# Tile 3's first layer begun on six ranked heads, paired up blocks for single tiles, and a new emission order

## The chip, the cores and the metric

One NeuronCore of a Trainium2 chip runs the whole program. The metric is the device time of one execution in microseconds (us), the median of several runs. Engines: TensorE (PE; its weight loads stand as PEld), VectorE (DVE), ScalarE (ACT), GpSimd (POOL) and SyncE (SP), which here only issues DMAs.

## What is computed

A top-32 attention over 8 heads, followed by two dense layers of width 2048 with a softplus between the first pair of matrices and a leaky ReLU between the second. All in float32; the weights arrive as float64 bit patterns that the kernel turns into float32 itself.

```python
scores = scale * np.matmul(q, k.transpose(0, 1, 3, 2))          # B,H,S,D = 2,8,576,64
kth = np.partition(scores, -32, axis=-1)[..., -32:-31]
scores = np.where(scores >= kth, scores, -1e9)
attn = np.exp(scores - scores.max(-1, keepdims=True))
x = np.matmul(attn / (attn.sum(-1, keepdims=True) + 1e-9), v)    # to 1152 x 512
h = x @ w_in;  x = (np.maximum(h, 0) + np.log1p(np.exp(-np.abs(h)))) @ w_out      # 512 -> 2048 -> 512
h = x @ w_in2; out = (np.maximum(h, 0) + alpha * np.minimum(h, 0)) @ w_out2
```

## The kernel before

The 1152 rows of tokens are 9 tiles of 128. `CHUNKS` groups them as [3], [4], [5], [6, 7, 8], [0, 1, 2]; below these are chunks 0 to 4. Chunks 0 to 2 run the first layer one tile at a time and the second layer together (`TOGETHER`); in these stages (`NATIVE`) the matrix products run in plain float32, which the trace shows as two matmuls per product. Chunks 3 and 4 split each float32 into a high and a low part and run three matmuls per product (`three`).

Per row (a tile and one head): `scores` makes the products on PE and copies them out on ACT. `topk` ranks on DVE: four MAX8 (L480) and three MATCH_REPLACE8 (L483) of 576 columns find the 32nd largest; then ACT or DVE makes the mask (L508 to L511), POOL subtracts it (L514), ACT takes the exponential (L516). `flip` transposes on PE, `values` multiplies by v on PE. When a tile's eighth head is through, `finish` takes the reciprocal of the sums on DVE, spreads it over the columns (POOL L606, PE L604, ACT L609) and one DVE product (L612) writes the tile's features `x` (called "x of tile t" below). Only then can the tile's first layer start.

`Layer.up(j)` makes block j (of 16) of the first matrix on PE from the four 128-row parts of x (L652 where float32), then three ACT instructions (L663 to L665: abs, exp, ln) and one DVE instruction (L666) make the softplus `g`; `Layer.down(j)` accumulates g times the second matrix on PE (L698, 512 columns). `convert` turns one unit of weights (two blocks, 1 MB of float64) into float32: two loads by SP, two DVE instructions (L351, L354), two of ACT (L357), four of POOL (L360), and a store for later reuse. The raw data lie in a ring of `RAWB` buffers, so a load waits until the unit `RAWB` before it has passed POOL.

All of this is first collected as 3208 numbered operations (`plan`), and then emitted in the order of the hand-written table `ORDER`; each engine, and SP's DMA queue, works in that order. An entry `fN` of the table emits N filler products of the identity with itself (L785, two matmuls each, 128 columns) on PE, whose result nobody reads. The 242 fillers all stand ahead of the first `up` block. A letter b behind an entry picks the operation's second engine (DVE for POOL, or DVE for ACT).

Of the kernel before, what the change touches and what calls it, by code (L numbers as in the profile page):

```python
# [8 lines left out]
F32 = mybir.dt.float32  # L9
# [9 lines left out]
P = 128  # L19
# [28 lines left out]
RAWB = 2  # L48
RING = 15
NATIVE = {(0, 1), (0, 2), (1, 2), (0, 0)}  # L50
HOLD = {(0, 1): 2, (0, 2): 4}

# [99 lines left out]
4 2 3 5 12 364 363 386 387 240 f11 6 19 96 7 8 56 f3 9 195 95 11 10 156 40 77 f4 13 26 41 117 14 0 42 27 15 f3  # L152
16 28 18 43 17 365 79 366 80 29 367 44 370 30 368 388 369 31 45 371 403 f31 20 32 372 21 63 22 404 f3 23 33
373 64 25 389 24 34 f4 57 46 393 65 35 47 36 390 66 394 81 48 391 67 395 59 58 82 37 392 423 f19 60 68 49 1
422 38 61 83 396 62 50 39 258 69 51 119 70 120 f9 52 54 103 71 405 53 72 105 55 104 f8 78 406 73 84 410 106 74
85 411 407 107 412 f8 75 424 440 76 408 86 425 409 87 121 429 88 142 439 413 122 426 89 108 430 143 123 90 427
109 431 f27 91 124 93 428 92 459 110 94 432 f4 97 125 111 458 118 441 99 112 98 144 100 126 113 135 145 101
127 442 114 146 128 446 158 129 f11 115 147 159 443 447 160 448 148 102 130 444 181 476 116 149 445 f14 131
182 161 133 150 475 460 449 132 151 162 134 f8 136 461 152 157 163 462 203 465 183 463 164 464 137 204 184 138
466 494 153 f10 139 477 467 174 185 141 140 478 468 f4 154 495 165 479 186 155 226 480 166 205 481 227 187 482  # L160
167 511 206 168 188 483 169 207 484 189 242 f26 170 172 485 228 171 190 512 173 208 243 f4 175 191 229 196 177
197 496 192 198 497 176 199 f2 178 209 498 230 219 501 499 210 231 500 179 180 244 502 f11 193 211 530 200 513
503 194 265 201 514 212 266 504 531 245 515 232 213 518 202 516 246 f18 380 517 214 381 233 519 374 547 382
# [136 lines left out]
def topk_attention_moe_kernel(ctx: ExitStack, tc: tile.TileContext, q, k, v, w1, w2, w3, w4, alpha, out):  # L300
# [185 lines left out]
    def topk(i):  # L486
        ci, ti, t, h = rows[i]
        if h == 0:
            tiles[t]["sum"] = buf("sum", 2, [P, H], F32, f"sum{t}")
# [348 lines left out]
```

## Time and profile before

| | us |
|---|---|
| median of 3 runs (lowest, highest) | 666.4 (665.17, 666.89) |
| the profiled execution | 665.31 |
| its span, first to last instruction | 663.5 |
| PE busy / DVE busy / ACT busy / POOL busy | 646.6 / 543.2 / 496.7 / 376.0 |

The span is 1.8 us shorter than the execution's own time. A PE shown as busy may still be waiting between two matmuls, since ends of matmuls are modelled; where this matters, starts are compared with starts.

### The profile page before, as it was taken

To read this page: it belongs to the slowest core of one execution; us is meant where nothing else is said; L and a number is where in the kernel's file an instruction comes from. 1 tells how busy PE (TensorE), PEld (TensorE's weight loads), DVE (VectorE), ACT (ScalarE), POOL (GpSimd) and SP (SyncE) were. 2 spreads that over 40 slices of the span, in tenths; PEclk is the share of its full clock that TensorE was granted. 3 is DMA by queue.
4 is the path that set the end of the run, shared out by engine and by line. 5 is a ranking of instruction groups with operands and counts; after the bars stand their busy time and mean duration, and the time that the engine had idled before them with its cause. 6 is when DMAs were issued, how large, how long until landed. Compare 5 with 4: busy or idle time off the path is not lost.

```text
span 663.5 us, 12370 instructions
## 1 busy us (share of the span) xinstructions
PE 646.6 (97%) x4340; PEld 501.7 (76%) x4340; DVE 543.2 (82%) x1046; ACT 496.7 (75%) x1118; POOL 376.0 (57%) x402
## 2 busy tenths in 40 slices
PE   9999998999999899999999999999999999999997
PEld 7899865667667554555567878878988999999886
DVE  4999999999999999999998889999744654664632
ACT  4778799898799978888788889888554667763532
POOL 1567766651343667887675769887643443652520
PEclk9999999899999999999999999999999999999999
DMA  8776787740044378857615322221233434432401
GB/s 294 251 213 214 227 252 256 254 144 1 1 130 142 112 221 271 283 184 230 211 64 156 100 89 85 83 69 61 95 126 128 147 124 128 157 130 96 159 1 47
DMA packets 30014, 98.46 MB, mean 148 GB/s; under 512 B 3456, under 2 KB 3968, under 8 KB 29952
## 3 DMA queue, kind: packets, MB, share of 16 engines
q1 hardware_dynamic: 29952, 97.67, 45.1%
q8 instruction: 34, 0.56, 0.3%
q14 instruction: 28, 0.23, 0.1%
HBM read 78.52 MB, written 19.14 MB: 147 GB/s over the span
## 4 chain that ended last, share of the span: by engine, by line
PE 74%; DVE 7%; issue 5%; ACT 5%; POOL 5%; DMA 3%; SPq 0%; POOLq 0%; DVEq 0%
PE pa L698 8%; PE ph L624 7%; PE pa L624 7%; PE ph L625 7%; PE ph L626 7%; PE pa L625 7%; PE pa L626 7%; PE scrap L785 7%; PE ph L652 6%; PE pss L471 5%; PE pp L529 3%; POOL cx L360 3%; DMA cr<-in_w_dram 3%; DVE r L483 2%; DVE m L480 2%
## 5 line engine op out<-in xcount | busy, mean ns | idle before, releaser
L370 POOL TENSOR_TENSOR w<-w,wh 128x512 fp32r<-128x512 f32 x82 | 126.7, 1555 | 101.4 <-ACT wh L393 93.7
L514 POOL TENSOR_TENSOR e<-s,e 128x288 f32<-128x288 f32 x144 | 120.0, 854 | 62.6 <-ACT e L509 57.4
L480 DVE MAX8 m<-r 128x8 f32<-128x576 f32 x216 | 155.4, 745 | 0.1
L360 POOL TENSOR_TENSOR cx<-cx,cr 128x256 int32<-128x256 int32 x128 | 93.6, 756 | 68.3 <-ACT cr L357 66.7
L483 DVE MATCH_REPLACE8 r<-m,r 128x576 f32<-128x576 f32 x144 | 106.1, 740 | 0.0
L698 PE MATMUL pa<-cx,g 128*128 128x512 f32 x188 | 94.5, 613 | 3.0 <-DVE g L666 2.6
L357 ACT ACTIVATE cr<-cr 128x512 int16<-128x512 uint32 x64 | 82.6, 1378 | 7.8 <-DVE cr L354 7.6
L393 ACT CAST wh<-w 128x1024 fp32r<-128x1024 f32 x64 | 66.8, 1045 | 6.4 <-PE pa L624 2.0
L476 ACT COPY s<-pss 128x288 f32<-128x288 f32 x144 | 53.3, 407 | 20.3 <-PE pss L471 19.7
L785 PE MATMUL scrap<-ident 128*128 128x128 f32 x484 | 60.9, 283 | 1.4 <-POOL ident masks.py:199 1.4
L785 PEld LDWEIGHTS scrap<-ident 128*128 128x128 f32 x484 | 57.4, 196 | 6.3 <-issue 4.9
L480 DVE MAX8 m<-s 128x8 f32<-128x576 f32 x72 | 52.6, 747 | 11.3 <-ACT s L476 11.3
L516 ACT ACTIVATE e<-e,nb 128x576 f32<-128x576 f32 x72 | 55.7, 774 | 5.6 <-POOL e L514 5.4
L624 PE MATMUL pa<-w,gh 128*128 128x512 f32 x144 | 59.0, 409 | 0.0
L371 DVE TENSOR_TENSOR w<-w,wh 128x512 fp32r<-128x512 f32 x46 | 37.2, 811 | 25.7 <-ACT wh L393 24.2
L625 PE MATMUL pa<-wh,gl 128*128 128x512 f32 x144 | 56.8, 395 | 0.0
L626 PE MATMUL pa<-wh,gh 128*128 128x512 f32 x144 | 56.8, 395 | 0.0
L471 PE MATMUL pss<-ks,q 64*64 64x288 f32 x576 | 53.3, 428 | 2.5 <-ACT pt L532 2.4
L672 DVE SCALAR_TENSOR_TENSOR g<-g,rest,ph 128x384 f32<-128x384 f32 x48 | 29.1, 607 | 31.6 <-ACT g L670 31.5
L670 ACT ACTIVATE g<-ph 128x384 f32<-128x384 f32 x48 | 23.3, 487 | 42.3 <-PE ph L626 37.7
L371 DVE TENSOR_TENSOR gl<-g,gh 128x384 fp32r<-128x384 f32 x41 | 42.2, 1028 | 15.1 <-ACT gh L679 14.9
L652 PEld LDWEIGHTS ph<-xh,cx 128*128 128x128 f32 x336 | 42.5, 193 | 15.1 <-issue 9.2
(130 smaller groups left out, 1459.5 us busy)
## 6 DMA issues: line engine op xcount, KB each, us to landing
w<-ws SPq DMA_DIRECT2D x67, 512.0 KB, 3.3
cr<-in_w_dram SPq DMA_DIRECT2D x64, 512.0 KB, 5.4
ws<-cx SPq DMA_DIRECT2D x32, 512.0 KB, 6.5
v<-in_v_dram SPq DMA_DIRECT2D x12, 320.0 KB, 6.9
ks<-in_k_dram SPq DMA_DIRECT2D x11, 288.0 KB, 5.7
out_dram<-o SPq DMA_DIRECT2D x9, 256.0 KB, 2.1
q<-in_q_dram SPq DMA_DIRECT2D x8, 256.0 KB, 5.3
ks<-in_k_dram SPq DMA_DIRECT2D x2, 144.0 KB, 2.8
```

The lines of the kernel that those rows point to most:

```text
L357: op("ACT", lambda r=r: nc.scalar.activation(r().bitcast(I16)[:, :, 2], r()[:, :, 0], AF.Copy, scale=2.0 ** -29), reads=[part], writes=[r])
L360: op("POOL", lambda part=part, r=r, cs=cs: nc.gpsimd.tensor_add(part().bitcast(I32)[:, cs], part().bitcast(I32)[:, cs], r().bitcast(I32)[: ...
L370: lambda: nc.gpsimd.tensor_sub(lo(), x(), hi().bitcast(F32)),
L471: nc.tensor.matmul(pss[n]()[part], qr()[head, pair, part], ks()[head, cs], start=True, stop=True)
L480: op("DVE", lambda: nc.vector.max(out=out(), in_=x()), reads=reads, writes=writes)
L483: op("DVE", lambda: nc.vector.match_replace(out=out(), in_to_replace=found(), in_values=x(), imm_value=LOWEST), reads=reads, writes=writes)
L514: op("POOL", lambda cs=cs: nc.gpsimd.tensor_sub(e()[:, cs], s()[:, cs], e()[:, cs]), reads=[s], writes=[e])
L624: nc.tensor.matmul(acc, ah, b_l, start=first, stop=False)
L625: nc.tensor.matmul(acc, a_l, bh, start=False, stop=False)
L626: nc.tensor.matmul(acc, ah, bh, start=False, stop=last)
L698: nc.tensor.matmul(acc(), gh()[:, cs], w[0]().bitcast(F32), start=first, stop=last)
L785: plan.emit(ORDER, lambda: nc.tensor.matmul(scrap()[:, :P], ident, ident, start=True, stop=True))
```

## The change

1. `STREAM = 6`: for tile 3 the sums and reciprocals are made in two parts (`finish_part`), after head 5 and after head 7. The products of the first three parts of x for all 16 blocks (`ahead`, 16 entries of 6 matmuls) go to PSUM, four blocks to a bank, and ACT copies them out (4 copies of 512 columns). Later each `up` block adds this partial sum by a product with the identity (2 matmuls) and its last part of x (2 matmuls), where it had 8 matmuls before.
2. `wide`: in the first layer of chunks 0 to 2 two `up` blocks share a PSUM bank, and abs, exp, ln and the DVE step run once on 256 columns instead of twice on 128.
3. `RAWB` 2 to 3. The weight tiles' ring is the same.
4. The first queries are loaded from ACT's DMA queue, ahead of the load of the activation table; the second half of the first scores takes its PSUM from another pool.
5. The 128x1 scaling of the row maximum may run on POOL (29 of 72 do).
6. The last stage's outputs: of its three tiles one is copied whole by ACT, one whole by DVE, and the last in halves into two buffers, each with its own DMA, one from ACT's queue and one from SP's (before: each tile in halves into one buffer, one DMA by SP).
7. `ORDER` is new: 3120 operations and 249 fillers. Entries ahead of three points of it:

| ahead of the point, before / after | PE | DVE |
|---|---|---|
| first `up` block of chunk 0; x of tile 3 (after: its last part) | fillers 242 / 249, `ahead` 0 / 16, flips of a head 9 / 10, middle flips 4 / 5, spreads 4 / 4 transposes, scores 14 / 14, values 4 / 4 | conversions' first step 9 / 13, second step 9 / 12, MAX8 46 / 49, MATCH_REPLACE8 34 / 36, x 0 / 1, sums and reciprocals 2 / 4 |
| first `up` block of chunk 1; x of tile 4 | fillers 242 / 249, scores 24 / 22, values 9 / 8, `down` of chunk 0 14 / 16, `up` of chunk 0 128 / 64 matmuls, `ahead` 0 / 96 matmuls, transposes of the finished tile 0 / 1 entry (4 matmuls) | conversions 16+16 / 16+16, MAX8 78 / 79, MATCH_REPLACE8 60 / 60, softplus step 14 of 128 / 8 of 256 columns, x 1 / 2, sums and reciprocals 4 / 6 |

In the order after, the 16 `ahead` entries stand behind the last value product of tile 3 (head 7), and between its last spread and the first `up` block stand 21 fillers. The DVE's first step of unit 14 of the weights (the 13th to be converted) stands just ahead of the last part of x of tile 3; its second load stands behind 14 of the 16 `ahead` entries, and so do the last POOL additions of unit 11, whose raw buffer it takes. Between the spread of tile 4 and the first `up` block of chunk 1 stand three entries of PE (before: 11).

```diff
-RAWB = 2
+RAWB = 3
+STREAM = 6
@@ prepare_q
-        for cs in (slice(0, 1), slice(1, 4)) if begin else (slice(0, 4),):
+        if begin:
+            def first():
+                nc.scalar.dma_start(qr()[:, :1], q[:, t][:, :1])
+                nc.scalar.preload_act_table_set("natural_log_exp_and_others")
+            op("ACT", first, writes=[Half(qr, 0, 1)])
+        for cs in (slice(1, 4),) if begin else (slice(0, 4),):
@@ finish_part (new; the chain of finish for heads lo to h)
+        op("PE", spread, reads=[rx], writes=[pr])
+        op("ACT", lambda: nc.scalar.copy(xn()[:, cols], pr()[:, cols]), reads=[pr], writes=[xn])
+        op("DVE", lambda: nc.vector.tensor_tensor(
+            x()[:, ks].rearrange("p k n -> p (k n)"), av()[:, cols], xn()[:, cols], op=ALU.mult),
...
@@ Layer
+        def ahead(self, j, z):
+            lo = j % 4 * P
+            self.products(j, j, z, slice(lo, lo + P), 0, STREAM // 2, [z], True)
+            if j % 4 == 3:
+                o = self.sums[j // 4]
+                op("ACT", lambda: nc.scalar.copy(o(), z()),
...
+                for i in range(self.wide):
+                    k, cols = (j + i) % 4 * P, slice(i * P, (i + 1) * P)
+                    self.products(j + i, at + i, hp, cols, STREAM // 2, KT, [hp], False, Half(o, k, k + P))
+                self.activate(j, at, n, nm, ci, hp, [hp])
...
+                    if base is not None:
+                        nc.tensor.matmul(hp()[:, cols], ident, base(), start=True, stop=False)
@@ the last stage's last tile
                     op("ACT", lambda o=o, acc=acc: nc.scalar.copy(o()[:, :half], acc()[:, :half]),
+                       reads=[acc], writes=whole)
+                    op("ACT", lambda t=t, o=o: nc.scalar.dma_start(out[t * P:(t + 1) * P, :half], o()[:, :half]),
+                       reads=whole)
+                    op("DVE", lambda z=z, acc=acc: nc.vector.tensor_copy(z()[:, half:], acc()[:, half:]),
+                       reads=[acc], writes=[Half(z, 0, half), Half(z, half, DM)])
+                    op("SP", lambda t=t, z=z: nc.sync.dma_start(out[t * P:(t + 1) * P, half:], z()[:, half:]),
...
```

## Rows read from the trace of the kernel before

**Rows 1.** The page: the span.
```profile
span 663.5 us, 12370 instructions
```
**Rows 2.** Stretches: start:end in us, length, busy time (count) by engine, granted clock, DMA.
```profile
core 0: us, PE busy (x) PEld busy (x) DVE busy (x) ACT busy (x) POOL busy (x), PEclk, DMA share, GB/s
0.00:78.90 78.90, 77.48 (x721) 68.79 (x721) 70.07 (x138) 55.76 (x114) 43.90 (x61) 1.00 0.72 236
78.90:136.30 57.40, 50.69 (x462) 33.92 (x462) 55.89 (x123) 53.28 (x141) 36.07 (x49) 0.97 0.74 242
...
343.40:663.50 320.10, 316.05 (x1885) 277.79 (x1883) 216.51 (x365) 212.26 (x428) 174.03 (x141) 1.00 0.31 103
```
**Rows 3.** Timeline of DVE (start, length, instruction, count): start of ranking, x of tiles.
```profile
8.39 1.42 DVE L480 MAX8 m<-s 128x8 f32<-128x576 f32 x2 [8.39 <-ACT s L476]
...
73.33 1.00 DVE L351 TENSOR_SCALAR cx<-cr 128x1024 uint32<-128x1024 uint32 x1 [0.43 <-DMA cr<-in_w_dram]
...
77.55 0.68 DVE L612 TENSOR_TENSOR xh<-pav__424,xn 128x512 f32<-128x512 f32 x1
...
131.73 0.68 DVE L612 TENSOR_TENSOR xh<-pav__1006,xn 128x512 f32<-128x512 f32 x1
```
**Rows 4.** Timeline of PE: fillers, a flip, the first up block of chunk 0.
```profile
45.73 2.72 PE L785 MATMUL scrap<-ident 128*128 128x128 f32 x22
48.28 0.60 PE L529 MATMUL pp<-ident,e 128*128 128x128 f32 x4
...
78.88 1.38 PE L652 MATMUL ph<-xh,cx 128*128 128x128 f32 x10
```
**Rows 5.** Timeline of ACT: the end of the exponential of that flip.
```profile
47.71 0.18 ACT L516 ACTIVATION_READ_ACCUMULATOR e<-e,nb 128x1 f32 x1
```
**Rows 6.** Timeline of PE: down, up, scores, values; first up block of chunk 1.
```profile
116.73 1.02 PE L698 MATMUL pa<-cx,g 128*128 128x512 f32 x2
117.59 0.61 PE L652 MATMUL ph<-xh,cx 128*128 128x128 f32 x4
...
133.33 1.31 PE L557 MATMUL pav__1593<-pt,v 128*64 128x128 f32 x20
134.58 1.12 PE L698 MATMUL pa<-cx,g 128*128 128x512 f32 x2
135.63 0.71 PE L471 MATMUL pss<-ks,q 64*64 64x288 f32 x8
136.28 1.16 PE L652 MATMUL ph<-xh,cx 128*128 128x128 f32 x8
```
**Rows 7.** Groups of instructions: busy us, mean ns of one, idle before.
```profile
L480 DVE MAX8 m<-r 128x8 f32<-128x576 f32 x216 | 155.4, 745 | 0.1
...
L354 DVE TENSOR_SCALAR cr<-cr 128x1024 uint32<-128x1024 uint32 x32 | 24.5, 765 | 0.0
...
L666 DVE SCALAR_TENSOR_TENSOR g<-ph,g 128x384 f32<-128x384 f32 x32 | 17.7, 552 | 16.7 <-ACT g L665 16.4
...
L666 DVE SCALAR_TENSOR_TENSOR g<-ph,g 128x128 f32<-128x128 f32 x48 | 13.3, 278 | 2.9 <-ACT g L665 2.7
```
**Rows 8.** Timeline of SP's DMA queue: the second load of one unit of weights.
```profile
67.01 0.42 SPq L348 DMA_DIRECT2D cr<-in_w_dram  x1
```
**Rows 9.** Waits of DVE from 135 to 350: total us, times, longest.
```profile
DVE cx L351 <- DMA cr<-in_w_dram: 4.2, 5, 1.3
```
**Rows 10.** Timeline of the end: last matmul, last two copies; DMA issues.
```profile
659.38 0.40 PE L626 MATMUL pa<-wh,gh 128*128 128x512 f32 x1
...
659.81 0.42 DVE L729 COPY o<-pa 128x256 f32<-128x256 f32 x1 [0.28 <-PE pa L626]
660.27 0.37 ACT L727 COPY o<-pa 128x256 f32<-128x256 f32 x1 [0.33 <-DVE o L729]
```
**Rows 11.** DMA issues of the page: count, KB each, us to landing.
```profile
out_dram<-o SPq DMA_DIRECT2D x9, 256.0 KB, 2.1
```
**Rows 12.** A stretch with a lower granted clock (columns as in rows 2).
```profile
125.00:135.00 10.00, 10.00 (x71) 7.05 (x70) 8.49 (x19) 8.26 (x25) 3.81 (x6) 0.87 0.57 204
```

More of the change, by code (lines that the diff above doesn't have):

```diff
@@ L151 @@
 ORDER = """
[L152 to L161, printed above, removed]
@@ L463, in scores @@
             cs = slice(half * HS, (half + 1) * HS)
-            pss = [bank(*(("pacc", 3) if ci == 0 else ("pt", 2)), HS, f"pss{t}{h + n}{half}") for n in range(2)]
+            pss = [bank(*(("pacc", 3) if ci == 0 and i + half != 1 else ("pt", 2)), HS, f"pss{t}{h + n}{half}") for n in range(2)]
             def products(cs=cs, pss=pss):
@@ L487, in topk @@
         ci, ti, t, h = rows[i]
-        if h == 0:
-            tiles[t]["sum"] = buf("sum", 2, [P, H], F32, f"sum{t}")
-        total = tiles[t]["sum"]
+        if h == 0 or streamed(ci) and h == STREAM:
+            tiles[t]["sum"] = buf("sum", 2, [P, H], F32, f"sum{t}{h}")
+        total = work[i]["sum"] = tiles[t]["sum"]
         s = work[i].pop("s")
@@ L498, in topk @@
         best(eight(0), s, [s], [m])
-        op("ACT", lambda: nc.scalar.mul(nb(), m()[:, 0:1], -SCALE), reads=[m], writes=[nb])
+        op(("ACT", "POOL"), (lambda: nc.scalar.mul(nb(), m()[:, 0:1], -SCALE), lambda: nc.gpsimd.tensor_scalar(
+            nb(), m()[:, 0:1], -SCALE, None, op0=ALU.mult)), reads=[m], writes=[nb])
         for n in range(1, 4):
@@ L586, in to_features, with streamed, finish_part, spread @@
                reads=[pp, hi], writes=[lo])
+    def streamed(ci):
+        return ci == 0 and STREAM
+    def finish_part(ci, t, h):
+        lo = STREAM if h == H - 1 else 0
+        n = h + 1 - lo
+        ks = slice(lo // 2, (h + 1) // 2)
+        if not lo:
+            x = features("x", ci, 0)[0]
+            xs[ci] = [(x, f"x{c}") for c in range(KT)]
+        x = xs[ci][0][0]
+        av, total = tiles[t]["av"], work[rows.index((ci, 0, t, h))]["sum"]
+        rs = buf("rs", 2, [P, H], F32, f"rs{t}{h}")
+        op("DVE", lambda: nc.vector.tensor_scalar(rs()[:, lo:h + 1], total()[:, lo:h + 1], 1e-9, None, op0=ALU.add),
+           reads=[total], writes=[rs])
+        op("DVE", lambda: nc.vector.reciprocal(rs()[:, lo:h + 1], rs()[:, lo:h + 1]), writes=[rs])
+        xn = buf("xn", XNB, [P, DM], F32, f"xn{t}{h}")
+        rx = buf("rx", 1, [P, H, D], F32, f"rx{t}{h}")
+        pr = bank("pt", 2, KT * P, f"pr{t}{h}_")
+        cols = slice(ks.start * P, ks.stop * P)
+        def spread():
+            for c in range(ks.start, ks.stop):
+                nc.tensor.transpose(pr()[:, c * P:(c + 1) * P], rx()[:, 2 * c:2 * c + 2, :].rearrange("p a b -> p (a b)"), ident)
+        op("POOL", lambda: nc.gpsimd.tensor_copy(
+            rx()[:, lo:h + 1], rs()[:, lo:h + 1].unsqueeze(2).broadcast_to([P, n, D])), reads=[rs], writes=[rx])
+        op("PE", spread, reads=[rx], writes=[pr])
+        op("ACT", lambda: nc.scalar.copy(xn()[:, cols], pr()[:, cols]), reads=[pr], writes=[xn])
+        op("DVE", lambda: nc.vector.tensor_tensor(
+            x()[:, ks].rearrange("p k n -> p (k n)"), av()[:, cols], xn()[:, cols], op=ALU.mult),
+           reads=[Half(av, c * P, c * P + P) for c in range(ks.start, ks.stop)] + [xn] + [x] * (lo > 0),
+           writes=[f"x{c}" for c in range(ks.start, ks.stop)] + [x] * (lo == 0))
     def finish(ci, ti, t):
@@ L639, in __init__ @@
             self.turned = layer == 0 and ci == len(CHUNKS) - 1 and len(among[ci]) == 1 and not self.native
+            self.wide = GROUP if self.native and layer == 0 and self.n == P else 1
             self.g = {}
-        def up(self, j, at):
-            n, nm, ci = self.n, f"{self.layer}{self.ci}_{j}", self.ci
+            self.early = streamed(ci) and layer == 0
+            if self.early:
+                self.sums = [buf("row", OB, [P, DM], F32, f"h{i}") for i in range(FJ // 4)]
+                for j in range(FJ):
+                    if j % GROUP == 0:
+                        fetch((layer, j // GROUP, 0), j, ci, True)
+                    if j % 4 == 0:
+                        z = bank("pacc", 3, 4 * P, f"pe{j // 4}")
+                    self.ahead(j, z)
@@ new lines, in ahead, with up_block @@
+        def ahead(self, j, z):
[4 more added lines that the diff above has]
+                op("ACT", lambda: nc.scalar.copy(o(), z()),
+                   reads=[z], writes=[Half(o, i * P, i * P + P) for i in range(4)])
+        def up(self, j, at):
+            if at % self.wide:
+                return
+            self.up_block(j, at)
+        def up_block(self, j, at):
+            n, nm, ci = self.n * self.wide, f"{self.layer}{self.ci}_{j}", self.ci
+            if self.early:
+                hp, o = bank("ph", 2, n, f"ph{nm}"), self.sums[j // 4]
+                for i in range(self.wide):
+                    k, cols = (j + i) % 4 * P, slice(i * P, (i + 1) * P)
+                    self.products(j + i, at + i, hp, cols, STREAM // 2, KT, [hp], False, Half(o, k, k + P))
+                self.activate(j, at, n, nm, ci, hp, [hp])
+                return
+            hp = bank("ph", 2, n, f"ph{nm}")
+            for i in range(self.wide):
+                self.products(j + i, at + i, hp, slice(i * self.n, (i + 1) * self.n), 0, KT, [hp])
+            self.activate(j, at, n, nm, ci, hp, [hp])
@@ L644, in up, with products @@
+        def products(self, j, at, hp, cols, c_lo, c_hi, writes, ahead=False, base=None):
+            n, ci = self.n, self.ci
             w = [x.parts[j % GROUP] for x in ready[self.layer, j // GROUP, 0]]
-            hp = bank("ph", 2, n, f"ph{nm}")
-            step = 1 if at == 0 and self.x[0] is not self.x[-1] else 2
-            for c0 in range(0, KT, step):
+            step = c_hi - c_lo if ahead else 1 if at == 0 and self.x[0] is not self.x[-1] or (c_hi - c_lo) % 2 else 2
+            for c0 in range(c_lo, c_hi, step):
@@ L651, in products, with activate @@
                         if self.native:
-                            nc.tensor.matmul(hp(), w[0]().bitcast(F32)[:, cs], self.x[c][0]()[:, c, :],
-                                             start=c == 0, stop=c == KT - 1)
+                            nc.tensor.matmul(hp()[:, cols], w[0]().bitcast(F32)[:, cs], self.x[c][0]()[:, c, :],
+                                             start=base is None and c == 0, stop=c == c_hi - 1)
                         else:
                             xh, xl, *_ = self.x[c]
-                            three(hp(), w[0]()[:, cs], w[1]()[:, cs], xh()[:, c, :], xl()[:, c, :],
+                            three(hp()[:, cols], w[0]()[:, cs], w[1]()[:, cs], xh()[:, c, :], xl()[:, c, :],
                                   c == 0, c == KT - 1)
-                op("PE", products,
-                   reads=w + [x for c in range(c0, c0 + step) for x in self.x[c][-2:]], writes=[hp])
+                op("PE", products if not ahead else lambda f=products: f(),
+                   reads=w + [x for c in range(c0, c0 + step) for x in self.x[c][-2:]] + [base] * (base is not None),
+                   writes=writes)
+        def activate(self, j, at, n, nm, ci, hp, made):
             g = buf("g", GB, [P, n], F32, f"g{nm}")
             if self.layer == 0:
-                op("ACT", lambda: nc.scalar.activation(g(), hp(), AF.Abs), reads=[hp], writes=[g])
+                op("ACT", lambda: nc.scalar.activation(g(), hp(), AF.Abs), reads=made, writes=[g])
                 op("ACT", lambda: nc.scalar.activation(g(), g(), AF.Exp, scale=-1.0), writes=[g])
```

210 lines of the change are left out of this document (130 added, 80 removed), and 108 rows, old and new, of the table ORDER.

## Prediction, made before the changed kernel was run

> **What bounds the kernel now.** I read the page first. The span is 663.5 us [rows 1], and PE is shown as busy for nearly all of it, but that share misleads: the fillers count as work. So I cut the span at the first `up` block of each chunk and read the table by stretches [rows 2]. Up to 78.9 us PE runs its 242 fillers and little else, and DVE, once it has something to rank (8.39 us, [rows 3]), is busy for 70.07 us of the remaining 70.5: DVE ranks without a pause. From 78.9 to 136.3 (chunk 0) DVE is busy for 55.89 of 57.40 us, while PE has matmuls in flight for only 50.69. From 343.4 to the end PE is busy for 316.05 of 320.10 us and DVE for 216.51. So the kernel has two ends. First DVE's queue decides when PE gets real work; later PE's own work decides, and a microsecond that PE loses early is never won back. The time is thus what PE must run, plus what it waits or fills up to the point from which it has always something to run, plus the tail. I take the first `up` block of chunk 1, 136.28 us [rows 6], as the point at which to compare: ahead of it DVE is full, behind it PE has little slack.
>
> **PE's work, counted.** Prices are starts against starts. Two runs of matmuls: 22 filler matmuls from 45.73 to 48.28 us give 0.116 us per float32 matmul of 128 columns, so 0.23 per filler [rows 4]. A `down` takes 0.86 (116.73 to 117.59), one half of a pair of scores 0.65 (135.63 to 136.28), a value product of a pair of heads 1.25 (133.33 to 134.58) [rows 6].
> In total the change adds 7 fillers (1.6 us) and the 16 identity products (32 matmuls, 3.7 us): 5.3 us. The 96 matmuls of `ahead` and the 64 late ones are otherwise the old 128. Ahead of the compared point PE has 7 fillers (+1.6), 32 matmuls (+3.7), 2 `down` (+1.7) and 4 transposes (+0.5) more, and 2 halves of scores (-1.3) and one value product (-1.25) less: +4.9. Behind it +0.4 is left. So with equal waits behind the point, the kernel is level if the first block of chunk 1 starts at 135.9.
>
> **DVE's queue up to that point.** Per instruction I take the group's mean less 0.08, since two MAX8 in a row last 1.42 us [rows 3] and one 0.745 [rows 7]: MAX8 0.67, a conversion step 0.69, a softplus step 0.20 at 128 columns and, between 0.20 and 0.47 (384 columns), 0.33 at 256. Up to x of tile 4 the new queue has one MAX8 (+0.67), one more x and its two small steps (+0.7 at most, each x being partial), and 8 wide softplus steps for 14 narrow ones (2.6 for 2.8). That is +1.2: x of tile 4 would start at 132.9 instead of 131.73 [rows 3], if nothing else changes. The ranking, 60 MATCH_REPLACE8 and 16 conversions, is the same; `ahead` needs nothing of DVE. DVE starts at about the same time: the 6 additional fillers ahead of the first scores (1.4 us at least) are made up by the second scores following at once, where 3 fillers (0.7) and a wait for a bank stood; the first queries' earlier issue is hidden behind these fillers, so I cost it at nothing (at worst, uncovered, 0.5 us).
>
> **What DVE may have to wait for.** The new order converts 13 units of weights up to the last x of tile 3 instead of 9. A load may start when the unit three before has passed POOL. Unit 14 takes the buffer of unit 11, whose last additions stand behind 14 of the 16 `ahead` blocks. PE reaches its first late block 13.2 us later than its counterpart before: 7 fillers 1.6, 96 matmuls 11.0, a flip and a middle flip 0.6; so near 92 us, and those 14 blocks near 84. The second load of a unit before was issued at 67.01 [rows 8] and its conversion started at 73.33, having waited for it for 0.43 us [rows 3]: 6.3 us. So unit 14's conversion, which stands just ahead of x of tile 3, can start at 90, while DVE's queue would reach it at 77.55 plus 7 conversion steps (4.8), 3 MAX8 and 2 MATCH_REPLACE8 (3.4) and 0.9 of small steps: 86.7. That is a wait of about 3.5 us. The fillers say the same: before, a run of fillers ends just after what the next instruction waits for (exponential done at 47.89 [rows 5], flip at 48.28 [rows 4]; x done at 78.23 [rows 3], block at 78.88 [rows 4]), so their number is a record of an expected wait, and the new one holds the first late block until 92. Bounds for this wait: 0 (the load comes in time, and only fillers are wasted) and 5.5 (92 less 86.7). I take 3.5, the value from the row of the load. Behind a waiting DVE stand ranking and every softplus step, so x of tile 4 goes to 136.4, ends at 137.1, and the first block of chunk 1, which has hardly other work ahead of it in PE's queue, starts at 137.3: 1.4 us later than level.
>
> **Behind that point.** Pairing takes 24 of 48 groups of ACT and DVE instructions out of chunks 0 to 2, and the third raw buffer lets loads start a unit earlier. From 135 to 350 us DVE waited 4.2 us in all for such loads [rows 9]. Bounds of the gain: 0 (PE had other work then) and 4.2; I take 2, since DVE and PE both have small gaps there. POOL gets 29 small scalings and ACT loses them; neither is full in these stretches [rows 2], so nothing for that, and as ACT's work falls the four copies of partial sums are covered; uncovered they stand at the last `ahead` bank only, some 0.5 us.
> The tail: the last matmul ends at 659.78, DVE copies to 660.23, and ACT, which writes the same buffer, starts only at 660.27 [rows 10]. With two buffers both copy at once: -0.4, at worst 0. The other two tiles' whole copies end before the last matmul. The last transfer is halved; a 256 KB one lands in 2.1 us [rows 11], and I give the halving 0.1.
> The Trainium skill (DMA: Bandwidth & Descriptors, section Anatomy of one DMA) has 2.0 us fixed per transfer and the bytes at 436 GB/s; an estimate by that is 0.3 us for the half that is saved, and the sum would be 0.2 lower. The row's 2.1 us for all 256 KB leaves less room than that formula, so this trace doesn't bear it out in full.
>
> Sum: +1.4 - 2 - 0.5 = -1.1 us against the profiled 665.31, that is 664.2; the median of the runs shown lies 1.1 above the profiled execution, so **665.3** on their scale. A measurement of this kernel can tell about 0.3%, 2.0 us, from no change.
>
> **Rivals.**
> *The loads come in time and the gaps behind close (faster).* If DVE waits for no load, x of tile 4 starts at 132.9, the first block of chunk 1 at 133.8, 2.1 ahead of level; with 2 to 4.2 won behind it and 0.5 at the end, -4.6 to -6.8: about 660.7. For it: three buffers give each load a whole unit's time more; DMA engines are busy for 0.72 to 0.74 of the time up to 136.3 [rows 2], not full. Against it: 13 units by 87 us for 9 by 78 are 4 MB of loads and 2 MB of stores more, 69 GB/s on top of 236, which would raise that share to 0.93.
> *DVE starves on loads (slower).* The same traffic, with the reloads and stores, makes the early conversions late not once but at several units from unit 2 on. DVE is full from 8.39 on, so each microsecond of it moves x of tile 4 alike. It decides from 6.6 us of such waits on (3.5 + 3.1), where the sum passes +2.0; at 8 us it is +3.4: 669.8.
> *The early start isn't early (slower).* All `ahead` blocks stand behind tile 3's last value product; if PE could not have run late blocks sooner anyway, the 5.3 us are added and nothing is saved, only the tail: +4.8, 671.2. For it: the first late block comes 13 us later than the first block did. Against it: the late blocks are 64 matmuls for 128, so chunk 0 then needs 7.4 us less of PE while DVE feeds it.
> *The clock falls.* Between 125 and 135 us the granted clock was 0.87 [rows 12], 0.97 over chunk 0 [rows 2]: PE had fallen from 2.4 to 1.2 GHz for about 0.03 x 57.4 x 2 = 3.4 us after waiting for softplus steps, which costs half of that, 1.7 us. The new order leaves PE waiting for x of tile 4 for some microseconds with three entries in between; a second fall makes the sum +0.6: 667.0. The Trainium skill (TensorE: Matmul & The Clock Gate, section HAM oscillation) warns that a gap in PE's work lets the clock drop; the stretch with 0.87 agrees.
>
> **How the numbers follow.** Forecast 665.3, chance 0.42; its own span is 663 to 668 (load wait 2 to 5.5 us, gain behind 1 to 3), of which 0.10 is faster by over 0.3%, 0.30 within, 0.02 slower. Loads in time 0.30 (faster). Starving 0.12 and no early start 0.12 (slower). The clock 0.04 (within). So faster 0.40, same 0.34, slower 0.26. Range 659.5 to 671.2: from loads in time with the full gain behind to the late start; beyond lie worse starving and gains not thought of.
>
> **What would show it.** DVE's wait ahead of unit 14's conversion near 87 to 90 us (right: about 3 us of waits for loads up to there; wrong: none, or many from 20 us on); x of tile 4 near 136; PE's first block of chunk 1 within a microsecond of its end; the softplus step of 256 columns near 0.41 us; DVE's waits for loads from 135 to 350 below 4.2; the last two copies side by side. If the first block of chunk 1 starts before 134 or after 139, the sum is wrong at DVE's queue; if it starts near 137 and the time still differs by over 3 us, it is wrong behind it.

## The result and the profile after

| | before | after |
|---|---|---|
| median of 4 runs (lowest, highest), us | 665.78 (662.87, 666.89) | 672.18 (670.63, 673.67) |
| ratio, 95% interval | | 1.0104 [1.0077, 1.0131] |
| the profiled execution, us | 665.31 | 673.67 |

The change made the kernel about 1% slower. My forecast of 665.3 was wrong, and so was its range, which ended at 671.2.

First the table by stretches, as in [rows 2], cut at the first late `up` block of chunk 0 (91.7), at the first block of chunk 1 (142.1), and from the first block of chunk 3 to the end. Columns: start:end, length, busy time of PE, PEld, DVE, ACT, POOL (instructions), granted clock, DMA share, GB/s.

```profile
0.00:91.70 91.70, 90.35 (x835) 82.08 (x835) 74.04 (x145) 63.49 (x121) 54.42 (x78) 1.00 0.76 246
91.70:142.10 50.40, 42.77 (x364) 27.17 (x364) 50.37 (x105) 43.97 (x99) 29.10 (x42) 0.93 0.71 250
358.50:671.90 313.40, 308.60 (x1850) 273.04 (x1848) 205.86 (x354) 209.17 (x424) 169.25 (x144) 1.00 0.30 100
```

DVE is again full over chunk 0 (50.37 of 50.40 us). But ahead of it DVE is busy for 74.04 of 91.70 us; before it was 70.07 of 78.90. It stood still for 17.7 us (before 8.8), 9.3 of it at the start. DVE's timeline shows where, and what came of it (start, length, instruction; in brackets the idle time before it and what ended that):

```profile
9.32 1.42 DVE L482 MAX8 m<-s 128x8 f32<-128x576 f32 x2 [9.32 <-ACT s L478]
...
83.45 1.41 DVE L482 MAX8 m<-r 128x8 f32<-128x576 f32 x2
91.36 0.69 DVE L347 TENSOR_SCALAR cx<-cr 128x1024 uint32<-128x1024 uint32 x1 [6.50 <-DMA cr<-in_w_dram]
...
94.63 0.68 DVE L347 TENSOR_SCALAR cx<-cr 128x1024 uint32<-128x1024 uint32 x1
95.22 0.29 DVE L624 TENSOR_TENSOR xh<-pav__437,xn 128x128 f32<-128x128 f32 x1
...
141.37 0.68 DVE L654 TENSOR_TENSOR xh<-pav__1116,xn 128x512 f32<-128x512 f32 x1
...
184.89 0.67 DVE L654 TENSOR_TENSOR xh<-pav__1655,xn 128x512 f32<-128x512 f32 x1
```

Ranking starts at 9.32 (before 8.39, [rows 3]). At 84.86 DVE runs out of work and waits 6.50 us for a load. The instruction at 91.36 is the first conversion step of unit 13, one unit ahead of the one that I had named; unit 14's step, at 94.63, didn't wait. The last part of x of tile 3 comes at 95.22, x of tile 4 at 141.37 (before 131.73, forecast 136.4), x of tile 5 at 184.89. In all up to 145 us (engine, line, what it waited for: total, times, longest):

```profile
DVE m L482 <- ACT s L478: 10.1, 3, 9.3
DVE cx L347 <- DMA cr<-in_w_dram: 7.5, 2, 6.5
```

Why the load was late is seen on SP's DMA queue and on POOL. SP:

```profile
70.13 0.81 SPq L344 DMA_DIRECT2D cr<-in_w_dram  x2
70.98 0.43 SPq L360 DMA_DIRECT2D ws<-cx  x1
82.75 1.29 SPq L344 DMA_DIRECT2D cr<-in_w_dram  x3
84.10 0.42 SPq L360 DMA_DIRECT2D ws<-cx  x1
```

POOL:

```profile
74.63 4.02 POOL L356 TENSOR_TENSOR cx<-cx,cr 128x256 int32<-128x256 int32 x5
79.03 0.87 POOL L356 TENSOR_TENSOR cx<-cx,cr 128x256 int32<-128x256 int32 x1 [0.39 <-ACT cr L353]
80.47 1.56 POOL L517 TENSOR_TENSOR e<-s,e 128x288 f32<-128x288 f32 x2 [0.56 <-ACT e L512]
81.98 0.74 POOL L356 TENSOR_TENSOR cx<-cx,cr 128x256 int32<-128x256 int32 x1
```

SP issued nothing from 71.4 to 82.75. By `ORDER` the three loads at 82.75 are the first half of unit 14 and then the two halves of unit 13. Unit 14 takes the raw buffer of unit 11, whose last addition on POOL ended at 81.98 + 0.74 = 82.72; 0.03 us later the queue moves. Unit 13's own buffer, that of unit 10, had been free since 78.65 (the five additions from 74.63). So its loads stood 4.5 us behind a load for a later unit.

PE then waits for x and loses its clock:

```profile
91.75 0.49 PE L728 MATMUL ph<-h,ident 128*128 128x128 f32 x2
95.56 0.79 PE L732 MATMUL ph<-xh,cx 128*128 128x128 f32 x2 [3.32 <-DVE xh L624]
...
142.11 1.60 PE L732 MATMUL ph<-xh,cx 128*128 128x128 f32 x12 [0.40 <-DVE xh L654]
```

```profile
91.00:105.00 14.00, 10.62 (x90) 8.55 (x89) 13.64 (x26) 10.85 (x22) 8.53 (x11) 0.76 0.78 292
```

The first late block stands ready at 91.75, as forecast, and waits 3.32 us for x; the granted clock over the next stretch is 0.76, which is 1.2 GHz for about half of it. Of the four executions two had a mean clock of 0.994 or 0.995 (673.67 and 673.06 us) and two of 1.000 (670.63 and 671.31): those with the fall are 2.4 us slower in the mean, two against two.

**Where the time is, in one table.** With starts against starts, as in the prediction, each kind of PE instruction has a usual pitch. All of PE's work at that pitch is one column; the rest of the span is time in which PE waits, runs fillers, or works slower than that pitch. I split it at the first block of chunk 1. It is worked out from PE's rows of each trace and used below for all kernels; in the last two some work lies on the other side of the point, and the sums take that into account. Each row is one profiled execution. That of e13 was its fastest, 2.2 us below its median, so its row flatters it by about as much.

| kernel | PE's work | point, us | not work ahead of it | not work behind it | span |
|---|---|---|---|---|---|
| before | 558.4 | 136.3 | 75.3 | 29.9 | 663.5 |
| after | 561.9 | 142.1 | 77.9 | 32.1 | 671.9 |
| e1: unit 13's loads first | 561.9 | 136.6 | 72.3 | 33.3 | 667.6 |
| e3: and 11 opening fillers | 561.9 | 136.4 | 72.2 | 31.7 | 665.8 |
| e8: and another order from 61 us to the point | 561.9 | 132.7 | 68.5 | 33.2 | 663.6 |
| e12: and another order to the end, 136 operations on another engine | 561.9 | 129.8 | 69.8 | 28.5 | 660.2 |
| e13: as e12, another order | 561.9 | 126.5 | 67.8 | 28.0 | 657.7 |

The change has 3.6 us more of work for PE (forecast 3.7 for the identity products, without the fillers). What I got wrong is in the other two columns: I had forecast 73.0 ahead (137.3 less 64.3) and 27.4 behind, and found 77.9 and 32.1.

### The profile page after: what moved, and what is told of

Its sections match the earlier page's. It is cut to its first block, busy times and chain, and to the rows that moved or that the text cites. A ratio compares the mean times of both kernels' runs of the same rounds, so it can differ in the third digit from the quotient of the medians.

```text
span 671.9 us, 12329 instructions
## 1 busy us (share of the span) xinstructions
PE 652.6 (97%) x4386; PEld 509.4 (76%) x4386; DVE 536.1 (80%) x1017; ACT 492.6 (73%) x1033; POOL 383.0 (57%) x433
## 4 chain that ended last, share of the span: by engine, by line
PE 79%; DVE 8%; ACT 4%; DMA 4%; POOL 3%; issue 2%; SPq 0%; DVEq 0%; POOLq 0%
PE ph L732 9%; PE pa L782 8%; PE scrap L880 7%; PE pa L666 7%; PE ph L666 7%; PE ph L667 7%; PE ph L668 7%; PE pa L668 6%; PE pa L667 6%; PE pss L473 6%; DMA cr<-in_w_dram 4%; PE pp L532 3%; DVE m L482 3%; DVE r L485 2%; POOL cx L356 1%
## 5 line engine op out<-in xcount | busy, mean ns | idle before, releaser
L366 POOL TENSOR_TENSOR w<-w,wh 128x512 fp32r<-128x512 f32 x81 | 123.0, 1528 | 96.1 <-ACT wh L389 95.3
L356 POOL TENSOR_TENSOR cx<-cx,cr 128x256 int32<-128x256 int32 x128 | 97.2, 780 | 50.0 <-ACT cr L353 47.1
L782 PE MATMUL pa<-cx,g 128*128 128x512 f32 x192 | 93.1, 601 | 2.4 <-POOL cx L356 1.5
L880 PEld LDWEIGHTS scrap<-ident 128*128 128x128 f32 x498 | 59.5, 198 | 4.6 <-issue 3.2
L512 ACT ACTIVATE e<-s,kb 128x576 f32<-128x576 f32 x70 | 54.4, 777 | 2.3
L782 PEld LDWEIGHTS pa<-cx,g 128*128 128x128 f32 x192 | 32.4, 190 | 29.7 <-issue 23.9
L485 DVE MATCH_REPLACE8 r<-m,s 128x576 f32<-128x576 f32 x72 | 53.1, 741 | 0.0
```

The lines of the kernel that those rows point to most:

```text
L356: op("POOL", lambda part=part, r=r, cs=cs: nc.gpsimd.tensor_add(part().bitcast(I32)[:, cs], part().bitcast(I32)[:, cs], r().bitcast(I32)[: ...
L366: lambda: nc.gpsimd.tensor_sub(lo(), x(), hi().bitcast(F32)),
L485: op("DVE", lambda: nc.vector.match_replace(out=out(), in_to_replace=found(), in_values=x(), imm_value=LOWEST), reads=reads, writes=writes)
L782: nc.tensor.matmul(acc(), gh()[:, cs], w[0]().bitcast(F32), start=first, stop=last)
L880: plan.emit(ORDER, lambda: nc.tensor.matmul(scrap()[:, :P], ident, ident, start=True, stop=True))
```

## The experiments

**e1: unit 13's loads ahead of unit 14's.** Entries on SP's queue alone; nothing else is touched.

```diff
 # ORDER, SP: 565 = first load of unit 14, 547 and 546 = the loads of unit 13
-565 547 546
+547 546 565
```

> The changed kernel with one move in SP's order: the two loads of weight unit 13 stand ahead of the first load of unit 14 instead of behind it. Theory A (SP's queue is in order, and the load of unit 14 waits for the whole raw buffer of unit 11, so unit 13's loads, whose buffer was free 4.1 us earlier, wait behind it): DVE's 6.5 us wait ahead of unit 13's conversion falls below 1.5, x of tile 4 moves from 141.4 to near 136.5, the time from 672.2 to 666 to 667.5. Rival B (the transfers themselves are slow, there is too much traffic at 80 to 90 us): the wait stays over 4 us and the time within 1 us of 672.2.

Measured 668.74 us (667.75 to 669.96), ratio to before 1.0034 [1.0018, 1.0050]; after had 1.0104. On SP the first two of the three loads now go at 78.05, right as unit 10's additions end, and only the third waits, again for unit 11:

```profile
78.05 4.40 SPq L342 DMA_DIRECT2D cr<-in_w_dram  x3
```

```profile
84.16 0.72 DVE L345 TENSOR_SCALAR cx<-cr 128x1024 uint32<-128x1024 uint32 x1
...
89.40 0.69 DVE L345 TENSOR_SCALAR cx<-cr 128x1024 uint32<-128x1024 uint32 x1 [1.86 <-DMA cr<-in_w_dram]
90.02 0.28 DVE L622 TENSOR_TENSOR xh<-pav__437,xn 128x128 f32<-128x128 f32 x1
...
135.84 0.69 DVE L652 TENSOR_TENSOR xh<-pav__1116,xn 128x512 f32<-128x512 f32 x1
```

Unit 13 no longer waits, unit 14 waits 1.86 us, x of tile 4 comes 5.5 us earlier than in after, and the granted clock stays at 1.00 from 91 to 105 us. One misplaced load was about two thirds of the loss, with the fall of the clock that it set off. It wasn't all of it: 668.74 lies above the 666 to 667.5 that I expected, and the span is 4.3 us shorter where the point came 5.5 us earlier.

**e3: and the old number of opening fillers.**

```diff
 # ORDER of e1, PE: fillers ahead of the first scores
-f17
+f11
```

> As e1_load13_first, and 11 fillers instead of 17 ahead of the first scores. Theory A (fillers hold the first scores: they end at 7.5, and ranking starts at 9.3 instead of 8.4; DVE is full from there to x of tile 4): ranking starts by 8.7, x of tile 4 0.6 to 0.9 us earlier than in e1_load13_first, the time 0.5 to 0.9 lower than its. Rival (the first keys and queries land that late): no change of the start, same time as e1_load13_first.

Measured 667.29 us (665.66 to 669.65), ratio 1.0021 [1.0005, 1.0037]. The gain over e1 in medians is 1.45 us, more than expected, but the intervals overlap. The start is told better by all the traces: with 17 fillers DVE started at 9.32, 8.67 and 9.86 us (after, e1, e4), with 11 at 8.64, 7.58, 8.33, 8.17, 8.64, 8.07 and 7.20 (e3, e7, e8, e9, e11, e12, e13): means 9.28 and 8.09. So in the mean the six fillers cost 1.2 us of start. The single starts lie far apart, and e1's is as early as e3's. The pitch of the opening matmuls shows why: it is 0.213 us at first and 0.112 later, and it changes at another moment in each execution.

**e4 and e7: no early start.** In after (e4) and in e3 (e7) the `ahead` entries and their copies emit nothing, and each late block makes all four parts of x; 32 matmuls fewer.

```diff
         def ahead(self, j, z):
-            self.products(j, j, z, slice(lo, lo + P), 0, STREAM // 2, [z], True)
+            op("PE", lambda: None, writes=[z])
 ...
-                    self.products(j + i, at + i, hp, cols, STREAM // 2, KT, [hp], False, Half(o, k, k + P))
+                    self.products(j + i, at + i, hp, cols, 0, KT, [hp])
```

> The changed kernel with its order, but the 16 early blocks and their 4 copies are left out, and each late block makes all four parts itself (8 matmuls instead of 4): TensorE has 32 matmuls (3.7 us) less in all. Theory A (up to x of tile 4 DVE's queue sets the time, TensorE has room): first block of chunk 1 stays within 1 us of 142.1, time within 1.5 us of 672.2. Rival B (the early start pays): 4 to 7 us slower, as 64 matmuls more follow x of tile 3. Rival C (the identity products are on the path): 3 to 4 us faster.

> As e3_load13_fill11 with the early blocks left out as in e4_no_ahead. Theory A: within 1.5 us of e3_load13_fill11, since DVE's queue still sets x of tile 4. Rival B (with the loads in time the early start pays): 3 to 7 us slower than e3_load13_fill11. Rival C: 3 to 4 us faster.

e4 took 679.11 us, 1.0185 [1.0156, 1.0214]; e7 672.41, 1.0090 [1.0068, 1.0112]. So without the early start the new order is 5 to 7 us slower, and my theory that it pays nothing falls. The stretch from the late blocks to the point, in e3 and then in e7, shows why:

```profile
91.00:136.40 45.40, 40.04 (x366) 24.82 (x365) 45.40 (x97) 41.44 (x96) 28.28 (x41) 1.00 0.72 246
```

```profile
92.00:140.70 48.70, 44.98 (x414) 30.18 (x412) 44.86 (x92) 40.50 (x92) 26.04 (x39) 1.00 0.63 212
```

In e3 DVE is busy for every microsecond of it and PE for 40.04 of 45.40. With the full late blocks, 64 matmuls more, PE is busy for 44.98 of 48.70 and DVE has 3.8 us of gaps, 2.9 of them ahead of softplus steps, whose chain starts at a late block:

```profile
DVE g L745 <- ACT g L744: 2.9, 2, 2.0
```

So DVE is no longer full there, and x of tile 4 comes at 140.00 instead of 135.65. In e7 PE was also idle or at 1.2 GHz for part of 72 to 92 us (granted clock 0.74), where the early blocks had stood, but its late blocks still came at the same time as those of e3. This is the value of the early start within the new order, which ranks tile 3's last heads later; it isn't a gain over the kernel before.

**e8: another order up to the point.** The instructions of e3 from the loads of unit 011 to the first block of chunk 1, permuted on all queues: x of tile 3's last part right after its spread, tile 4's chain and the conversions ahead of tile 5's ranking, 36 fillers fewer. The order was found by a small program that replays the queues with the durations of e3's trace. It isn't a permutation alone: six scalings of a row maximum change places between ACT and POOL, three each way, and on SP's queue one load changes places at about 32 us already. (The fillers of the stretch fall from 47 to 11; the 61 in the text on record is a miscount.)

> The kernel of e3 (loads of unit 013 first, 11 opening fillers), with all instructions between the loads of unit 011 (about 61 us) and the first up block of chunk 1 put into another order on their queues, and the fillers of that stretch cut from 61 to 11; the same instructions otherwise, and nothing changed behind that point. x of t3's last two heads is made at about 80 us instead of 90, so that the late blocks follow the early ones without fillers, and the conversions of units 013 to 017 and the last heads of tile 4 stand earlier. Theory 'PE's queue': from the first late block (91.1 in e3) to the first block of chunk 1 (136.4) PE was at work for some 40 of 45 us, so the point follows the first late block: late blocks from 80 to 85, point at 127 to 131, median 659 to 663. Theory 'DVE's queue' (my prediction's): DVE had no gap there in e3, so x of tile 4 stays near 135 and the median near 666 to 668. If the early start cannot be worth more than e3 shows, 667.

Measured 665.64 us (664.48 to 668.38), ratio 1.0011 [0.9994, 1.0027]: between the two expectations. The point moved by 3.7 us, less than that was left at the end. DVE's rows say why:

```profile
82.23 0.28 DVE L621 TENSOR_TENSOR xh<-pav__431,xn 128x128 f32<-128x128 f32 x1
...
129.51 0.68 DVE L651 TENSOR_TENSOR xh<-pav__1147,xn 128x512 f32<-128x512 f32 x1
...
177.91 0.67 DVE L651 TENSOR_TENSOR xh<-pav__1613,xn 128x512 f32<-128x512 f32 x1
```

The last part of x of tile 3 comes 8.2 us earlier than in e3 (90.40), x of tile 4 6.1 earlier (135.65), but x of tile 5 only 1.3 earlier (179.17). DVE's queue is full through both rankings; to bring tile 4 forward is to push tile 5 back, and PE, early at chunk 1, waits more there (47.5 us from its first block to that of chunk 2, 45.1 in e3). So my theory of DVE's queue holds for a point one chunk later than the one at which I compared, and the first block of chunk 1 was a poor place to compare orders.

**e9: the pairs undone in cost.**

```diff
-                op("ACT", lambda: nc.scalar.activation(g(), hp(), AF.Abs), reads=made, writes=[g])
+                cut = pieces(n, self.n if ci in (1, 2) else n)
+                op("ACT", lambda: [nc.scalar.activation(g()[:, cs], hp()[:, cs], AF.Abs) for cs in cut], ...)
 # and so for exp, ln and the DVE step
```

> The kernel of e3 with the pairs undone in cost alone: in chunks 1 and 2 each abs, exp, ln and multiply-add over 256 columns is given as two over 128 in the same places of the same queues (64 instructions more, 48 of them on ScalarE). My prediction took 2 us (0 to 4.2) for the pairs behind the point: by that 669.3 (667.3 to 671.5). Rival 'the pairs give nothing there, ScalarE has room': 667.3, within 0.7.

Measured 667.35 us (665.70 to 668.91), ratio 1.0039 [1.0023, 1.0055], where e3 had 1.0021: 0.0018 more, 1.2 us, with an uncertainty of about 1.5. That would lean to a worth of the pairs near my 2, but e11 (below), which ran beside e9 and differs from e3 in nothing that showed, has 1.0037 and 667.42 us. Against e11 the pairs are worth nothing that can be seen. The 667.35 us are also the rival's number and at the lower end of mine.

**e10: the pairs alone, in the kernel before.**

```diff
+            self.wide = GROUP if layer == 0 and ci in (1, 2) else 1
 ...
         def up(self, j, at):
-            hp = bank("ph", 2, n, f"ph{nm}")
+            if at % self.wide:
+                return
+            hp = bank("ph", 2, n * self.wide, f"ph{nm}")
+            for i in range(self.wide):
+                self.block(j + i, at + i, hp, slice(i * self.n, (i + 1) * self.n))
```

An operation whose inputs aren't emitted yet is held back until they are. On PE's queue that moves two half blocks by one place; the rest of it stands as before.

> The kernel before with one part of the change alone: two up blocks per activation in chunks 1 and 2, in the order of before, where the merged instructions come right after the second block of a pair. By my prediction 2 us faster than before (0 to 4.2): 663.9. Rival 'a merged activation makes the first block of each pair wait for the second, and the down blocks with it': 0 to 2 us slower than before.

Measured 680.50 us (680.20 to 681.97), ratio 1.0242 [1.0221, 1.0263]: 15 us slower, far outside both expectations. The stretch of chunks 1 and 2 is 14.8 us longer, which is all of it. From the first block of chunk 1 to the first of the second layer, before and then e10:

```profile
136.30:231.80 95.50, 92.87 (x713) 63.03 (x709) 93.74 (x212) 84.51 (x254) 39.88 (x53) 1.00 0.29 92
```

```profile
135.70:246.00 110.30, 96.68 (x712) 63.22 (x708) 93.91 (x196) 82.41 (x206) 39.78 (x53) 1.00 0.24 80
```

ACT is relieved by 2.1 us, and PE stands 13.6 us instead of 2.6. The largest sum of waits is that of `down` blocks for g; most of the rest are waits of flips and scores:

```profile
PE pa L711 <- DVE g L678: 4.6, 6, 1.0
PE pp L532 <- ACT s L479: 2.4, 1, 2.4
```

In an order that was written for single blocks, the first block of each pair has its g a block later, and `down` stands in front of PE's queue. That the other waits follow from these is argued from the order of the queue, not shown. The pairs and the order belong together: pairs show no worth in the new one (e9 against e11) and cost 15 us in the old.

**e11: the first queries by SP again.**

```diff
-                nc.scalar.dma_start(qr()[:, :1], q[:, t][:, :1])
-                nc.scalar.preload_act_table_set("natural_log_exp_and_others")
-            op("ACT", first, writes=[Half(qr, 0, 1)])
+            op("SP", lambda: nc.sync.dma_start(qr()[:, :1], q[:, t][:, :1]), writes=[Half(qr, 0, 1)])
```

> The kernel of e3 with the first queries fetched by SyncE's queue again, ahead of the keys, and the activation table loaded at the start. The first scores stand behind 11 fillers, which end at 6.3 us in e3; if the queries were there before that either way, nothing changes: 667.3 within 0.7. If ScalarE's queue had brought the first scores forward, ranking starts up to 0.5 us later: 667.8.

Measured 667.42 us (666.25 to 669.27), ratio 1.0037 [1.0020, 1.0054], the same as e3 within the intervals; ranking starts at 8.64 us in both profiles. The part does nothing, as I had costed it: the first scores wait for the fillers.

**e12 and e13: another order to the end.** The instructions of e3, permuted as for e8, from about 61 us to the end; 29 and 33 fillers fewer than e3. Both also give 136 operations to another engine than e3 does. Most are subtractions of a high part from a float32, of which DVE hands 21 and 22 more to POOL than it takes; the others are scalings of a row maximum between ACT and POOL, and 8 and 12 masks from ACT to DVE (one goes the other way in e13). So these runs try order and choice of engine together.

> The instructions of e8, put into another order on all queues from the loads of unit 011 (about 61 us) to the end; no other edit. In e8 the first block of chunk 1 came 3.7 us earlier than in e3, but PE then stood 2.4 us more in the stage of chunk 1, and only 2.1 us were left at the end; behind that point PE's matmuls end 527 us later in e8 and 525.7 in e3, of which some 498 are its own work at the usual pitch. Theory 'order': what the change loses behind the point is waits of the queues' new order, not a price of its parts; then the same instructions in an order that keeps ranking ahead of PE give 3 to 15 us back: 650 to 662. Theory 'price of the parts' (shared x buffers of chunks 3 and 4, pairs that arrive together, the identity products): no order gives it back: 663 to 668.

> As e12, another order found from e3's: the same expectation, 650 to 662 by 'order' and 663 to 668 by 'price of the parts'. If the two differ by more than 3 us, the gain hangs on single waits of one order and not on the stage as a whole.

Measured 662.51 us (660.94 to 663.43), ratio 0.9967 [0.9953, 0.9981], and 661.66 (659.48 to 665.17), 0.9967 [0.9948, 0.9985]: faster than the kernel before by 0.3%, and 0.44% faster than e8. Behind the point the time that isn't work falls from 33.2 (e8) to 28.5 and 28.0. That it is below the 29.9 of before isn't shown: these are single executions, and beside e12 and e13 the kernel before itself ran 1.5 us faster (664.33) than beside e1 to e7 (665.88). Of e3's waits of PE from 136.5 on the two largest are

```profile
PE pp L530 <- ACT s L476: 1.7, 3, 0.7
PE pss L471 <- ACT s L476: 1.1, 1, 1.1
```

and of e13's, from there on as well,

```profile
PE pa L663 <- POOL gl L363: 0.6, 1, 0.6
PE ph L663 <- DVE g L752: 0.2, 1, 0.2
```

In all, PE's waits that the view lists behind the point are 5.0 us in before, 6.8 in after, 6.4 in e3, 2.0 in e12 and 1.6 in e13. All parts of the change are still in e12 and e13, and also two things that its list leaves out (chunks 3 and 4 share the buffers of their x, and DVE makes 2 masks where it made 8). So the parts don't force the waits that came with the order of after. By my ranges the choice is less clear: 662.51 lies between the two and 661.66 just inside "order", and the kernel before was fast beside them too. How much of the gain is order and how much is choice of engine stays open.

**e14 and e15: the same treatment for the kernel before.** Its instructions, permuted in the same way; 44 and 59 fillers fewer, and 82 and 113 operations on another engine.

> The kernel before, its instructions unchanged, put into another order on all queues from the first loads of the second half of the weights to the end, found in the same way as the orders of e12 and e13; fillers cut from 242 to 198. If the 1.3 us that e12 and e13 lie under the kernel before come from the change's parts (early blocks, pairs, third raw buffer), this kernel stays at its 664 to 666, and the parts are worth about 1 to 3 us at orders of equal care. If they come from the order alone, it falls to 660 to 663 as they did, and the parts are worth nothing.

> As e14, another order of the same instructions, fillers 183: the same expectation. If the two differ by more than 3 us, no judgement on the parts is possible from them.

Measured 671.21 us, 1.0086 [1.0070, 1.0102], and 669.36, 1.0054 [1.0035, 1.0072]: both slower than before's own order and outside both expectations. PE's listed waits behind the point fall here too (3.6 and 2.3 us, 5.0 in before), so these waits aren't all that an order costs. The gain of e12 and e13 isn't what any such reordering gives. It doesn't show either that the kernel before has no better order; how much of the 0.3% is owed to the parts stays open.

## Why the prediction was wrong, step by step

Two terms failed, by about the same amount: the wait for loads ahead of the point (7.5 us in the place of 3.5), and the gain behind it (a loss of 2.2 us in the place of a gain of 2).

- *What bounds the kernel*: right up to the point. DVE's idle time early on came out at the first block of chunk 1 almost one for one: x of tile 4 was 5.0 us later than forecast and that block 4.8. Behind the point it was too simple. I took it that a microsecond lost or won at the point stays, but DVE's queue still holds PE in the next stage: the point came 5.5 us earlier in e1 than in after and the span was 4.3 shorter; in e8, against e3, it was 3.7 and 2.1.
- *PE's work, counted*: right, 3.6 us more beside the fillers.
- *DVE starts at about the same time*: wrong by 0.9 us in the profiled execution and 1.0 in the means (with before's opening ranking starts at 8.39, 8.33, 8.22 and 8.22 us in before, e10, e14 and e15). The first scores stand behind the opening fillers. Before and after:

```profile
5.64 0.72 PE L471 MATMUL pss<-ks,q 64*64 64x288 f32 x8
```

```profile
7.53 1.20 PE L473 MATMUL pss<-ks,q 64*64 64x288 f32 x16
```

  Of these 1.9 us the six more fillers took 1.4, as I had priced them, and the eleven ahead of them 0.5 more than before, since their pitch fell later. Both halves of the scores following at once won back 1.0, where I had let them win back everything.
- *What DVE may have to wait for*: this step failed. The mechanism was right (a load that waits for POOL's additions of the unit that held its buffer, with the conversion in front of DVE's queue), the unit was wrong. I followed unit 14's load to its buffer and asked when it would land; I didn't ask what stands behind it on SP's queue. Unit 13's loads did, though needed earlier. The waits were 7.5 us instead of 3.5. Of my bounds, 0 to 5.5, the upper end came from the fillers, that is from when the order expected to be served.
- *The rival "DVE starves on loads"* had its decision point at 6.6 us of waits and 669.8 us at 8; 7.5 were measured. It is the rival that came true in kind, with one blocked queue in the place of general traffic (the share of the DMA engines was 0.76 up to the first late block, not 0.93), and the terms behind the point made it dearer.
- *Behind that point*, -2: this step failed too, by 4.2 (the copies of the tail, below, are the rest of the 4.7). Taken by themselves the parts behave as forecast in after: the softplus step of 256 columns takes 410 ns (the view of groups by shape), and DVE's waits for loads from 145 to 355 us are 3.0 us, where [rows 9] had 4.2 for 135 to 350:

```profile
L749 DVE SCALAR_TENSOR_TENSOR g<-ph,g 128x256 f32<-128x256 f32 x24 | 9.7, 410 | 0.6 <-ACT g L748 0.3
```

```profile
DVE cx L347 <- DMA cr<-in_w_dram: 3.0, 3, 1.7
```

  In the place of a gain of 2 us PE's listed waits behind the point rose from 5.0 to 6.8. They are waits for single instructions, which a sum over groups can't see. They go in e12 and e13, whose time that isn't work is 1.4 and 1.9 us below that of before; but these are single executions, so a gain of my 2 isn't shown even there, and e9 against e11 shows none of the pairs. Before e10 I had no sign of how much this part depends on the order.
- *The tail*, -0.5: wrong; nothing was gained. The two halves have buffers of their own, and still one follows the other:

```profile
667.81 0.39 PE L668 MATMUL pa<-wh,gh 128*128 128x512 f32 x1
...
668.23 0.42 DVE L822 COPY oz<-pa 128x256 f32<-128x256 f32 x1 [0.67 <-PE pa L668]
668.68 0.33 SPq L824 DMA_DIRECT2D out_dram<-oz  x1
668.69 0.37 ACT L818 COPY o<-pa 128x256 f32<-128x256 f32 x1 [0.55 <-DVE oz L822]
669.09 0.35 ACTq L820 DMA_DIRECT2D out_dram<-o  x1
```

  From the start of the last matmul to the end of the span it is 4.09 us; before it was 4.12 ([rows 10], [rows 1]). I took the common output buffer for what held ACT back in [rows 10]; what the copies still share is the PSUM tile `pa`, and no run gave the halves tiles of their own. The Trainium skill (PSUM — Partial Sum Buffer, section PSUM bank collisions raise a hardware error) says that ScalarE and VectorE must not read one bank on the same partitions at once, at disjoint columns too, and that software has to order them; the two copies one behind the other agree.
- *The clock falls*: I gave it 0.04 and 1.7 us. It happened in two of four executions, for the reason given (PE waiting for x), at another place (tile 3's x, not tile 4's), and these two were 2.4 us slower.
- *Loads in time and gaps closed*, 660.7: not this kernel, but near what e12 and e13 come to (662.5 and 661.7) with loads, start, order and choice of engine changed.
- *The early start isn't early*: no; e4 and e7 put its worth at 5 to 7 us within the new order.

In sum, against before in ratios: after +1.04%; unit 13's loads put first, +0.34%; opening fillers as before, +0.21%; another order up to the point, +0.11%; another order and other engines up to the end, -0.33%. The first and the last of these steps are larger than their intervals; the two between are not each shown by themselves.

## What to carry to other kernels

A DMA that waits in an in-order queue holds all that is queued behind it, so for each load that may wait, read who stands behind it and when that is needed, not only when the load itself lands. Where one engine's queue is full through several stages, compare two orders at a point behind all of these stages: an earlier start of the next stage can be borrowed from the one after it. A part that merges instructions has no price of its own; it has one in an order made for it (here nothing that could be seen) and another in the old one (here a loss of 15 us).

## What the runs showed of the hardware that I had not expected

- Two engines that copied two halves of one PSUM tile into two different buffers ran one after the other (DVE to 668.65, ACT from 668.69, released by DVE's copy), as they did into one buffer before.
- The time of the opening moves from execution to execution: 22 filler matmuls lasted from 4.14 us (e13) to 5.06 (e3) and the first scores behind them 1.20 and 1.72, and ranking starts up to 1.4 us apart for the same program start. The pitch of the fillers has two levels, 0.213 us and 0.112, and goes from one to the other earlier in e13 than in e3. The view of the granted clock shows 1.00 there in both, so that the clock rises from 1.2 to 2.4 GHz at that moment is read from the pitch alone.
- The Trainium skill (TensorE: Matmul & The Clock Gate, section HAM oscillation) warns of gaps in PE's work; here a wait of 3.32 us was followed by a granted clock of 0.76 over 14 us in one execution, while two others of the same kernel, whose waits weren't traced, kept a mean clock of 1.000. In the kernel before, PE stood for 2.1 us behind the point without losing it.
